# Attention and two MLPs in one kernel: the second MLP's rational function written as P·r·(2 − Q·r) in one PSUM bank, and the accumulators copied out in the step of their last matmul

## The chip, the cores and the metric

The kernel runs on one core of one Trainium2 chip. The metric is the device time of one execution in microseconds (us). An execution's span is the time from its first to its last instruction in the trace. Engines are named as in the profile: PE is TensorE's matmuls, PEld its weight loads, DVE is VectorE, ACT is ScalarE, POOL is GpSimd, SP issues the DMAs.

## The reference

```python
# q, k, v: (8, 8, 576, 64); x below: 4608 tokens x 512
q_s = softmax(q, axis=-1);  k_s = softmax(k, axis=2)
x = einsum(q_s, einsum('bhsd,bhse->bhde', k_s, v))      # to (4608, 512)
# first MLP (d_ff = 2048)
h = x @ moe_w_in
x = (h - tanh(h)) @ moe_w_out
# second MLP, a rational function of h
h = x @ moe2_w_in
P = a[0] + a[1]*h + a[2]*h*h + a[3]*h*h*h
Q = 1.0 + abs(b[0])*abs(h) + abs(b[1])*h*h
return (P / (Q + 1e-06)) @ moe2_w_out
```

## The kernel before

Tokens are worked in 9 blocks (index j, NBLK) of 512, and the 2048 hidden features in 16 slices (index f, KF) of 128. The first MLP is phase 1 and the second is phase 2; each is one loop of 144 steps (n), a step being one slice of one block. Every product is made from float32r parts: a value is split into a high part (h) and a low part (l), and `mm3` issues high·high, high·low and low·high. So `first_product` is 12 matmuls into one PSUM bank `hps` (four chunks c of the input, three matmuls each), and `second_product1` or `second_product2` is 12 matmuls into the four accumulators `acc0` to `acc3` (three in a row each). The order of each engine's instructions is written by hand: an engine runs its own list in program order, and semaphores hold it where it needs another engine's result.

In step n the PE list has the first product of n and then the second product of n−2 (LAG1 and LAG2 are 2), which is taken from `due`. Between the two products of one slice stands the nonlinearity.

Phase 1: ACT makes tanh into `t` (L668), DVE subtracts (L669), ACT rounds to `gh` (L237) and POOL makes `gl` (L238). Beside it run the attention of the next block (functions named kv_ and q_, spread over the steps by `front`, `turn` and `follow`), and, in `park`, the decoding of phase 2's weights.

Phase 2, with one line per instruction of 128×512: ACT makes |b0 h| into the PSUM tile `rx` (L623) and h² into `h2` (L624); DVE makes `qq` = |b1|h² + rx (L625); ACT makes the numerator's two linear pieces `n1` and `n0` (L631, L632); POOL makes n1·h2 (L633) and n0 + n1 (L634). ACT makes a first reciprocal r in `rx` (L606, L607). DVE refines it by one Newton step (L611, L612), multiplies it by the numerator (L615), rounds that to `gh` (L237) and subtracts for `gl` (L238). The reciprocal and everything behind it of slice n is issued in step n+1.

At the end of a block two more pieces of work come up. In the step f = 15, `next_x` splits the next block's input: ACT rounds four chunks to `xh` (L224) and DVE subtracts for four chunks `xl` (L225), ahead of that step's other work. One step and a half later, after the last second product of the block, the closure `leave` copies `acc0` and `acc2` out on ACT (L570 in phase 1, L587 in phase 2) and `acc1` and `acc3` on DVE (L571, L588), and SP stores them. `leave` is returned by the second product, is called in the next step (under the name `end`), and the next block's second product can write an accumulator only when its copy is done.

Of the kernel before, what the change touches and what calls it, by code (L numbers as in the profile page):

```python
# [8 lines left out]
F32 = mybir.dt.float32  # L9
F32R = mybir.dt.float32r  # L10
# [4 lines left out]
AF = mybir.ActivationFunctionType  # L15
ALU = mybir.AluOpType
AX = mybir.AxisListType

P = 128
NB = 512  # L20
NEG = -3.0e38
EPS_S = 1e-9
ONE_EPS = 1.0 + 1e-6

SK = 32
LAG1 = 2
LAG2 = 2
# [3 lines left out]
def attention_moe_moe2_kernel(ctx, tc, q, k, v, w1, w2, w3, w4, ca, cb, out):  # L31
# [11 lines left out]
    NBLK = NT // NB  # L43
    NPAIR = H // 2
    KC = DM // P
# [8 lines left out]
    gp = ctx.enter_context(tc.tile_pool(name="gp", bufs=2))  # L54
# [5 lines left out]
    PE, ACT, DVE, POOL, SP = nc.tensor, nc.scalar, nc.vector, nc.gpsimd, nc.sync  # L60

    def f32(ap):
        return ap.bitcast(F32)
# [142 lines left out]
    def unpark(which, f):  # L206

        d = parked[which, f]
        for i, w in enumerate(place((which, f))):
            SP.dma_start(out=f32(w), in_=d[:, i])  # L210
# [7 lines left out]
    xh, xl = (xp.tile([P, KC, NB], F32R, tag=f"x{part}", name=f"x{part}") for part in "hl")  # L218
    xr = xp.tile([P, KC, NB], F32, tag="xr", name="xr")

    def next_x():

        for c in range(KC):
            ACT.copy(out=xh[:, c, :], in_=xr[:, c, :])  # L224
            DVE.tensor_tensor(out=xl[:, c, :], in0=xr[:, c, :], in1=f32(xh[:, c, :]), op=ALU.subtract)  # L225

    def first_product(f):
        hps = ps_h.tile([P, NB], F32, tag="h", name="hps")
# [2 lines left out]
            mm3(hps, wh, wl, xh[:, c, :], xl[:, c, :], c == 0, c == KC - 1)  # L231
        return hps

    def split(g, on_dve):
        gh = gp.tile([P, NB], F32R, tag="gh", name="gh")
        gl = gp.tile([P, NB], F32R, tag="gl", name="gl")
        (DVE.tensor_copy if on_dve else ACT.copy)(out=gh, in_=g)  # L237
        (DVE if on_dve else POOL).tensor_tensor(out=gl, in0=g, in1=f32(gh), op=ALU.subtract)  # L238
        return gh, gl

    acc = {}
# [245 lines left out]
    def follow(after):  # L487
        for fn in [late for fn in after for late in [fn()] if late]:
            fn()
# [21 lines left out]
    with tc.manual_schedule():  # L511
# [47 lines left out]
        def second_product1(j, f, gh, gl):  # L559
            if f == 0:  # L560
                new_acc()
            wh, wl = wb(f)
            for m in range(4):
                c = slice(m * P, (m + 1) * P)
                mm3(acc[m], wh[:, c], wl[:, c], gh, gl, f == 0, f == KF - 1)

            def leave(acc=dict(acc)):
                for m in range(0, 4, 2):
                    st = leaving()
                    ACT.copy(out=st[:, 0], in_=acc[m])  # L570
                    DVE.tensor_copy(out=st[:, 1], in_=acc[m + 1])  # L571
                    SP.dma_start(out=x2d[j][:, m:m + 2], in_=st)

            return leave if f == KF - 1 else None

        def second_product2(j, f, gh, gl):
            if f == 0:
                new_acc()
            wh, wl = wb(f)
            for m in range(4):  # L580
                c = slice(m * P, (m + 1) * P)
                mm3(acc[m], gh[:, c], gl[:, c], wh, wl, f == 0, f == KF - 1)

            def leave(acc=dict(acc)):
                for m in range(0, 4, 2):
                    st = leaving()
                    ACT.copy(out=st[:, 0], in_=acc[m])  # L587
                    DVE.tensor_copy(out=st[:, 1], in_=acc[m + 1])  # L588
                    rows = out[j * NB:(j + 1) * NB, :].rearrange("(p g) m -> p g m", g=4)
                    SP.dma_start(out=rows[:, m:m + 2], in_=st)  # L590

            return leave if f == KF - 1 else None
# [8 lines left out]
        ahead = const.tile([P, 1], F32, name="ahead")  # L601
        DVE.memset(bias_q, ONE_EPS * 2.0**-SK)

        def rational_seed(x, qq):

            ACT.activation(out=x, in_=qq, func=AF.Abs_reciprocal_sqrt, scale=2.0**-SK, bias=bias_q)  # L606
            ACT.activation(out=x, in_=x, func=AF.Square, scale=2.0 ** (-SK / 2))  # L607

        def rational_step(x, qq):

            DVE.scalar_tensor_tensor(out=qq, in0=qq, scalar=ONE_EPS, in1=x, op0=ALU.add, op1=ALU.mult)  # L611
            DVE.scalar_tensor_tensor(out=x, in0=qq, scalar=2.0, in1=x, op0=ALU.subtract, op1=ALU.mult)  # L612

        def rational_end(x, n0):
            DVE.scalar_tensor_tensor(out=n0, in0=n0, scalar=-1.0, in1=x, op0=ALU.mult, op1=ALU.mult)  # L615
            return split(n0, True)

        def rational_open(hps):

            x = ps_a.tile([P, NB], F32, tag="a", name="rx")  # L620
            h2 = rp.tile([P, NB], F32, tag="h2", name="h2")
            qq = rp.tile([P, NB], F32, tag="qq", name="qq")
            ACT.activation(out=x, in_=hps, func=AF.Abs, scale=b0)  # L623
            ACT.activation(out=h2, in_=hps, func=AF.Square)  # L624
            DVE.scalar_tensor_tensor(out=qq, in0=h2, scalar=b1, in1=x, op0=ALU.mult, op1=ALU.add)  # L625
            return x, h2, qq

        def rational_top(hps, h2):
            n1 = rp.tile([P, NB], F32, tag="n1", name="n1", bufs=1)
            n0 = rp.tile([P, NB], F32, tag="n0", name="n0")  # L630
            ACT.activation(out=n1, in_=hps, func=AF.Identity, scale=a3, bias=a2)  # L631
            ACT.activation(out=n0, in_=hps, func=AF.Identity, scale=a1, bias=a0)  # L632
            POOL.tensor_tensor(out=n1, in0=n1, in1=h2, op=ALU.mult)  # L633
            POOL.tensor_tensor(out=n0, in0=n0, in1=n1, op=ALU.add)  # L634
            return n0


        STEPS = NBLK * KF
        due = {}
        last = STEPS - KF  # L640
        rat = leave = None
        for n in range(2 * STEPS + LAG2 + 1):
            ph, j, f = n // STEPS, n % STEPS // KF, n % KF
            end, leave = leave, None
            if n < STEPS:
                front(work[n])
                hps = first_product(f)
                if end:
                    end()
                if f == KF - 1 and j + 1 < NBLK:  # L650
                    next_x()
                if n == last:
                    ACT.activation(out=absb, in_=coef[:, 4:6], func=AF.Abs)
                    att.release()
                    outp = ctx.enter_context(tc.tile_pool(name="outp", bufs=2, side="right"))
                    load_x2(0)
                if n >= last:
                    unpark("a", f)
                if f == KF - 1 and n > last:
                    next_x()  # L660
                    load_x2(1)
                if n in due:
                    leave = due.pop(n)()
                if n >= last + LAG1:
                    unpark("b", f - LAG1)
                after = turn(work[n])
                t = gp.tile([P, NB], F32, tag="t", name="t", bufs=1)
                ACT.activation(out=t, in_=hps, func=AF.Tanh)  # L668
                DVE.tensor_tensor(out=t, in0=hps, in1=t, op=ALU.subtract)  # L669
                ph_w, turns = None, 0  # L670
                if j == 0:
                    ph_w, turns = 0, 1 if f % 4 == 2 else 2
                due[n + LAG1] = lambda a=(j, f, *split(t, False)): second_product1(*a)
                if turns:
                    decode(ph_w, True)
                follow(after)
                if turns > 1:
                    decode(ph_w, False)
                if KF - 1 <= n < KF + PACE * (2 * KF + 1):
                    park(n - KF)  # L680
                if n == STEPS - 1:

                    ACT.activation(out=ahead, in_=bias_q, func=AF.Abs_reciprocal_sqrt)
            else:
                if n == STEPS:
                    rp = ctx.enter_context(tc.tile_pool(name="rp", bufs=2, side="right"))
                old, rat = rat, None
                if n < 2 * STEPS:
                    hps = first_product(f)
                    if f == KF - 1 and j + 1 < NBLK:  # L690
                        next_x()
                        if j + 2 < NBLK:
                            load_x2(j + 2)
                leave = due.pop(n)() if n in due else None
                if n < STEPS + LAG1:
                    unpark("b", KF - LAG1 + f)
                if old:
                    rational_seed(*old[0])
                if end:
                    end()  # L700
                if old:
                    rational_step(*old[0])
                if n < 2 * STEPS:
                    x, h2, qq = rational_open(hps)
                    rat = ((x, qq), rational_top(hps, h2), (j, f))
                if old:
                    due[n + LAG2 - 1] = lambda a=(*old[2], *rational_end(old[0][0], old[1])): second_product2(*a)


# [28 lines left out]
```

## Time and profile before

| | before |
|---|---|
| runs | 1741.19, 1742.47, 1742.45 us; median 1742.45 |
| profiled execution | 1741.09 us; span 1739.3 us |
| PE busy | 1686.4 us, 97% of the span |
| PEld, DVE | 1389.8 us (80%), 1221.4 us (70%) |
| ACT, POOL | 978.6 us (56%), 674.1 us (39%) |
| chain that ended last | PE 84%, DVE 11%, issue 3%, ACT 1% |

The busy shares are means over both phases. In phase 1 (up to about 930 us) DVE is busy about half of the time; in phase 2 (from about 930 us) over nine tenths. An idle bracket in the rows below, as [0.95 <-DVE gl L238], is the time that the engine sat idle before the instruction and who ended the wait. Names in the rows leave out buffer numbers, and matmuls of several weight slices can share a name.

### The profile page before, as it was taken

How to read it: one execution, taken by the hardware profiler on the slowest of the kernel's cores; microseconds unless marked ns; L12 is line 12 of the kernel's file. 1: busy time of each engine (PE TensorE's matmuls, PEld its weight loads, DVE VectorE, ACT ScalarE, POOL GpSimd, SP SyncE). 2: the span in 40 equal slices, each digit the busy share in tenths (PEclk: the TensorE clock that was granted, in tenths of full speed). 3: DMA queues.
4: the chain of work that ended last, by engine and by line, in shares of the span. 5: the costliest groups of instructions: out<-in, count | busy, mean ns of one | idle time of the engine just before them, and what ended most of it. 6: DMA issues, size and time to landing. Idle time of an engine off the chain costs nothing.

```text
span 1739.3 us, 21473 instructions
## 1 busy us (share of the span) xinstructions
PE 1686.4 (97%) x7640; PEld 1389.8 (80%) x7640; DVE 1221.4 (70%) x1785; ACT 978.6 (56%) x1656; POOL 674.1 (39%) x544
## 2 busy tenths in 40 slices
PE   5899999999999999999999999999999999999998
PEld 3677888888888888888888878787878787878786
DVE  7997445455444545432215999999999999999997
ACT  5666444444444444432325676767676767676765
POOL 3443323233222323233223444444444444444443
PEclk8899999999999999999999999999999999999999
DMA  7552433333332333210354010101010101000000
GB/s 214 159 161 69 135 95 112 94 105 106 100 98 89 119 100 106 74 55 1 131 194 159 0 49 1 49 1 49 1 49 1 49 1 46 4 31 19 1 25 24
DMA packets 108763, 125.13 MB, mean 72 GB/s; under 512 B 48624, under 2 KB 82416, under 8 KB 107504
## 3 DMA queue, kind: packets, MB, share of 16 engines
q1 hardware_dynamic: 108656, 123.76, 22.2%
q8 instruction: 60, 0.98, 0.2%
q14 instruction: 47, 0.39, 0.1%
HBM read 88.08 MB, written 35.65 MB: 71 GB/s over the span
## 4 chain that ended last, share of the span: by engine, by line
PE 84%; DVE 11%; issue 3%; ACT 1%; SPq 0%; DMA 0%; DVEq 0%; ACTq 0%
PE acc L68 14%; PE acc L66 13%; PE acc L67 13%; PE hps L68 13%; PE hps L66 13%; PE hps L67 13%; PE kvps L359 2%; DVE e L134 1%; DVE m L135 1%; DVE xl L225 1%; DVE m L122 1%; DVE gl L238 1%; PE qps L442 1%; DVE n L615 1%; DVE gh L237 1%
## 5 line engine op out<-in xcount | busy, mean ns | idle before, releaser
L238 POOL TENSOR_TENSOR gl<-t,gh 128x512 fp32r<-128x512 f32 x144 | 187.6, 1303 | 546.9 <-ACT gh L237 546.9
L633 POOL TENSOR_TENSOR n<-n,h 128x512 f32<-128x512 f32 x144 | 186.5, 1295 | 404.0 <-ACT n L631 404.0
L237 ACT CAST gh<-t 128x512 fp32r<-128x512 f32 x144 | 89.4, 621 | 291.5 <-PE acc L68 267.2
L669 DVE TENSOR_TENSOR t<-hps,t 128x512 f32<-128x512 f32 x144 | 98.9, 687 | 217.0 <-ACT t L668 217.0
L238 DVE TENSOR_TENSOR gl<-n,gh 128x512 fp32r<-128x512 f32 x144 | 213.9, 1485 | 13.7
L623 ACT ACTIVATE rx<-hps,coef 128x512 f32<-128x512 f32 x144 | 95.3, 662 | 210.0 <-PE hps L68 210.0
L634 POOL TENSOR_TENSOR n<-n,n 128x512 f32<-128x512 f32 x144 | 193.7, 1345 | 11.3
L668 ACT ACTIVATE t<-hps 128x512 f32<-128x512 f32 x144 | 85.9, 596 | 160.2 <-PE hps L68 159.7
L237 DVE CAST gh<-n 128x512 fp32r<-128x512 f32 x144 | 119.5, 830 | 14.1 <-PE acc L68 0.5
L625 DVE SCALAR_TENSOR_TENSOR qq<-h,absb,rx 128x512 f32<-128x512 f32 x144 | 107.5, 746 | 27.3 <-ACT h L624 14.7
L66 PE MATMUL hps<-xh,wa2h 128*128 128x512 f32 x288 | 115.5, 401 | 0.0
L68 PE MATMUL hps<-xh,wa3l 128*128 128x512 f32 x288 | 112.6, 391 | 2.9 <-DVE wa3l L146 2.9
L66 PE MATMUL hps<-xh,wa1h 128*128 128x512 f32 x288 | 115.1, 400 | 0.0
L66 PE MATMUL hps<-xh,wa3h 128*128 128x512 f32 x288 | 114.5, 398 | 0.0
L66 PE MATMUL hps<-xh,wa0h 128*128 128x512 f32 x288 | 114.4, 397 | 0.0
L632 ACT ACTIVATE n<-hps,coef 128x512 f32<-128x512 f32 x144 | 113.7, 789 | 0.0
L67 PE MATMUL hps<-xl,wa0h 128*128 128x512 f32 x288 | 113.0, 392 | 0.0
L68 PE MATMUL hps<-xh,wa0l 128*128 128x512 f32 x288 | 112.8, 392 | 0.0
L68 PE MATMUL hps<-xh,wa2l 128*128 128x512 f32 x288 | 112.5, 391 | 0.0
L67 PE MATMUL hps<-xl,wa2h 128*128 128x512 f32 x288 | 112.5, 391 | 0.0
L67 PE MATMUL hps<-xl,wa1h 128*128 128x512 f32 x288 | 112.4, 390 | 0.0
L631 ACT ACTIVATE n<-hps,coef 128x512 f32<-128x512 f32 x144 | 112.4, 780 | 0.0
(227 smaller groups left out, 4565.5 us busy)
## 6 DMA issues: line engine op xcount, KB each, us to landing
raw<-in_moe_w_in_dram SPq DMA_DIRECT2D x32, 512.0 KB, 4.2
raw<-in_moe_w_out_dram SPq DMA_DIRECT2D x32, 512.0 KB, 4.1
xr<-x2d SPq DMA_DIRECT2D x9, 1024.0 KB, 4.7
out_dram<-st SPq DMA_DIRECT2D x18, 512.0 KB, 2.7
kt<-in_k_dram SPq DMA_DIRECT2D x32, 256.0 KB, 2.9
vt<-in_v_dram SPq DMA_DIRECT2D x64, 128.0 KB, 3.0
x2d<-raw SPq DMA_DIRECT2D x14, 512.0 KB, 3.2
qr<-in_q_dram SPq DMA_DIRECT2D x8, 256.0 KB, 3.3
```

Of the source, the lines that this page charges most:

```text
L66: PE.matmul(o, lhi, rhi, start=start, stop=False)
L67: PE.matmul(o, lhi, rlo, start=False, stop=False)
L68: PE.matmul(o, llo, rhi, start=False, stop=stop)
L237: (DVE.tensor_copy if on_dve else ACT.copy)(out=gh, in_=g)
L238: (DVE if on_dve else POOL).tensor_tensor(out=gl, in0=g, in1=f32(gh), op=ALU.subtract)
L623: ACT.activation(out=x, in_=hps, func=AF.Abs, scale=b0)
L625: DVE.scalar_tensor_tensor(out=qq, in0=h2, scalar=b1, in1=x, op0=ALU.mult, op1=ALU.add)
L631: ACT.activation(out=n1, in_=hps, func=AF.Identity, scale=a3, bias=a2)
L632: ACT.activation(out=n0, in_=hps, func=AF.Identity, scale=a1, bias=a0)
L633: POOL.tensor_tensor(out=n1, in0=n1, in1=h2, op=ALU.mult)
L634: POOL.tensor_tensor(out=n0, in0=n0, in1=n1, op=ALU.add)
L669: DVE.tensor_tensor(out=t, in0=hps, in1=t, op=ALU.subtract)
```

## The change

Four things are rewritten.

1. The rational function. `rx` holds in turn |b0 h|, Q, Q·r and the quotient; `qq` is gone. The reciprocal's first value r goes to an SBUF tile `r`. POOL multiplies the numerator by r, DVE makes x = (Q + 1e-6)·r and then x = (x − 2)·n0 in the same PSUM bank; the coefficients of the numerator are negated once. DVE rounds the bank to `gh` and subtracts for `gl` from the bank. `n1` has two buffers. The reciprocal's ACT instructions and the product with r are issued in the slice's own step, behind the numerator; the last product and the split in the next step.
2. In the last step the numerator's three POOL instructions run on DVE.
3. In phase 2 `next_x` gives the subtractions of chunks 2 and 3 to POOL.
4. `leave` is called in the step of the last matmul, behind the split. In phase 2 all four copies are DVE's, save in the last block.

```diff
-    def next_x():
+    def next_x(low=None):
         for c in range(KC):
             ACT.copy(out=xh[:, c, :], in_=xr[:, c, :])
-            DVE.tensor_tensor(out=xl[:, c, :], in0=xr[:, c, :], in1=f32(xh[:, c, :]), op=ALU.subtract)
+            eng = (low or [DVE] * KC)[c]
+            eng.tensor_tensor(out=xl[:, c, :], in0=xr[:, c, :], in1=f32(xh[:, c, :]), op=ALU.subtract)
...
-                    ACT.copy(out=st[:, 0], in_=acc[m])
+                    (ACT.copy if j == NBLK - 1 else DVE.tensor_copy)(out=st[:, 0], in_=acc[m])
...
-            DVE.scalar_tensor_tensor(out=qq, in0=h2, scalar=b1, in1=x, op0=ALU.mult, op1=ALU.add)
...
+        def rational_q(x, h2):
+            DVE.scalar_tensor_tensor(out=x, in0=h2, scalar=b1, in1=x, op0=ALU.mult, op1=ALU.add)
+        def rational_seed(x):
+            r = rp.tile([P, NB], F32, tag="r", name="r")
+            ACT.activation(out=r, in_=x, func=AF.Abs_reciprocal_sqrt, scale=2.0**-SK, bias=bias_q)
+            ACT.activation(out=r, in_=r, func=AF.Square, scale=2.0 ** (-SK / 2))
+            return r
+        def rational_step(x, r, n0, eng):
+            eng.tensor_tensor(out=n0, in0=n0, in1=r, op=ALU.mult)
+            DVE.scalar_tensor_tensor(out=x, in0=x, scalar=ONE_EPS, in1=r, op0=ALU.add, op1=ALU.mult)
+        def rational_end(x, n0):
+            DVE.scalar_tensor_tensor(out=x, in0=x, scalar=2.0, in1=n0, op0=ALU.subtract, op1=ALU.mult)
+        def split_end(x):
+            gh, gl = parts()
+            DVE.tensor_copy(out=gh, in_=x)
+            DVE.tensor_tensor(out=gl, in0=x, in1=f32(gh), op=ALU.subtract)
+            return gh, gl
...
+                    DVE.tensor_scalar(out=coef[:, 0:4], in0=coef[:, 0:4], scalar1=-1.0, scalar2=None, op0=ALU.mult)
...
                 follow(after)
+                if leave:
+                    leave()
...
+                eng = DVE if n == 2 * STEPS - 1 else POOL
...
-                        next_x()
+                        next_x((DVE, DVE, POOL, POOL))
...
+                if n < 2 * STEPS:
+                    x, h2 = rational_open(hps)
                 if old:
-                    rational_seed(*old[0])
-                if end:
-                    end()
-                if old:
-                    rational_step(*old[0])
+                    rational_end(*old[0])
                 if n < 2 * STEPS:
-                    x, h2, qq = rational_open(hps)
-                    rat = ((x, qq), rational_top(hps, h2), (j, f))
+                    rational_q(x, h2)
+                    n0 = rational_top(hps, h2, eng)
                 if old:
-                    due[n + LAG2 - 1] = lambda a=(*old[2], *rational_end(old[0][0], old[1])): second_product2(*a)
+                    due[n + LAG2 - 1] = lambda a=(*old[1], *split_end(old[0][0])): second_product2(*a)
+                if leave:
+                    leave()
+                if n < 2 * STEPS:
+                    rational_step(x, rational_seed(x), n0, eng)
+                    rat = ((x, n0), (j, f))
```

## Rows read from the trace of the kernel before

**Rows 1.** Windows, 200 us of phase 2: busy us (instructions) by engine, clock, DMA.
```profile
1200.00:1400.00 200.00, 198.09 (x870) 162.35 (x869) 185.72 (x233) 140.96 (x231) 94.56 (x73) 1.00 0.07 27
```
**Rows 2.** Timeline of PE in phase 2: start, duration, instruction, idle before it.
```profile
1109.95 0.50 PE L68 MATMUL acc<-wb3h,gl 128*128 128x512 f32 x1 [0.95 <-DVE gl L238]
...
1197.13 0.40 PE L67 MATMUL acc<-wb3l,gh 128*128 128x512 f32 x1
1198.48 0.50 PE L68 MATMUL acc<-wb3h,gl 128*128 128x512 f32 x1 [0.95 <-DVE gl L238]
1198.82 0.40 PE L66 MATMUL acc<-wb3h,gh 128*128 128x512 f32 x1
...
1714.48 0.39 PE L66 MATMUL hps<-xh,wa3h 128*128 128x512 f32 x1
...
1719.92 0.39 PE L66 MATMUL hps<-xh,wa3h 128*128 128x512 f32 x1
```
**Rows 3.** Waits of PE, 950 to 1735 us: total us, times, longest.
```profile
PE acc L68 <- DVE gl L238: 8.6, 9, 1.0
```
**Rows 4.** Waits of PEld and of PE, 130 to 945 us.
```profile
PEld acc L66 <- DVE raw L571: 7.5, 6, 1.7
...
PE acc L66 <- DVE raw L571: 5.0, 4, 1.3
```
**Rows 5.** Timeline of PE in phase 1, at one of those waits.
```profile
665.24 0.39 PE L68 MATMUL acc<-gh,wb0l 128*128 128x512 f32 x1
666.84 0.50 PE L66 MATMUL acc<-gh,wb0h 128*128 128x512 f32 x1 [1.21 <-DVE raw L571]
```
**Rows 6.** Timeline of DVE in the same place.
```profile
662.25 0.29 DVE L332 TENSOR_REDUCE mc<-kvps 128x1 f32<-128x128 f32 x1 [1.45 <-PE kvps L326]
...
666.10 1.28 DVE L571 COPY raw<-acc 128x512 f32<-128x512 f32 x2
```
**Rows 7.** Groups by line, 800 to 1700 us: count, busy us, mean ns, idle before.
```profile
L634 POOL TENSOR_TENSOR n<-n,n 128x512 f32<-128x512 f32 x139 | 186.9, 1345 | 10.9
...
L625 DVE SCALAR_TENSOR_TENSOR qq<-h,absb,rx 128x512 f32<-128x512 f32 x139 | 103.7, 746 | 26.7 <-ACT h L624 14.7
...
L612 DVE SCALAR_TENSOR_TENSOR rx<-qq,rx 128x512 f32<-128x512 f32 x138 | 95.9, 695 | 4.7
```
**Rows 8.** Instructions of single lines: ns lowest/median/highest, first and last start.
```profile
L238 POOL TENSOR_TENSOR gl<-t,gh x144: 1276/1294/1837, 50.5 to 930.7; 128x512 fp32r<-128x512 f32 x144
L238 DVE TENSOR_TENSOR gl<-n,gh x144: 691/1594/1667, 941.7 to 1730.8; 128x512 fp32r<-128x512 f32 x144
...
L237 DVE CAST gh<-n x144: 427/841/1323, 940.8 to 1730.2; 128x512 fp32r<-128x512 f32 x144
...
L615 DVE SCALAR_TENSOR_TENSOR n<-n,rx x144: 677/681/687, 940.1 to 1729.4; 128x512 f32<-128x512 f32 x144
...
L588 DVE COPY st<-acc x18: 675/677/691, 1031.9 to 1735.0; 128x512 f32<-128x512 f32 x18
```
**Rows 9.** Timeline of ACT: a block's end, and the last step of phase 2.
```profile
1189.46 2.67 ACT L224 CAST xh<-xr 128x512 fp32r<-128x512 f32 x4 [0.89 <-PE hps L68]
...
1722.84 0.66 ACT L623 ACTIVATE rx<-hps,coef 128x512 f32<-128x512 f32 x1 [1.73 <-PE hps L68]
...
1723.90 0.78 ACT L631 ACTIVATE n<-hps,coef 128x512 f32<-128x512 f32 x1
1724.56 0.79 ACT L632 ACTIVATE n<-hps,coef 128x512 f32<-128x512 f32 x1
...
1725.96 0.58 ACT L607 ACTIVATE rx<-rx 128x512 f32<-128x512 f32 x1
```
**Rows 10.** Timeline of PE over the last two second products.
```profile
1726.38 0.50 PE L66 MATMUL acc<-wb3h,gh 128*128 128x512 f32 x1 [0.86 <-DVE gh L237]
...
1734.60 0.39 PE L68 MATMUL acc<-wb3h,gl 128*128 128x512 f32 x1
```
**Rows 11.** Windows, a stretch inside them: columns as in the first group.
```profile
1729.00:1732.00 3.00, 3.00 (x9) 2.32 (x8) 2.14 (x4) 0.00 (x0) 0.00 (x0) 0.50 0.00 0
```

More of the change, by code (lines that the diff above doesn't have):

```diff
@@ L232, in first_product, with parts, split @@
         return hps
[L234 to L238, printed above, removed]
+    def parts():
+        return tuple(gp.tile([P, NB], F32R, tag=tag, name=tag) for tag in ("gh", "gl"))
+    def split(g):
+        gh, gl = parts()
+        ACT.copy(out=gh, in_=g)
+        POOL.tensor_tensor(out=gl, in0=g, in1=f32(gh), op=ALU.subtract)
         return gh, gl
@@ L602, in attention_moe_moe2_kernel @@
         DVE.memset(bias_q, ONE_EPS * 2.0**-SK)
[L604 to L616, printed above, removed]
         def rational_open(hps):
@@ L621, in rational_open, with rational_top @@
             h2 = rp.tile([P, NB], F32, tag="h2", name="h2")
-            qq = rp.tile([P, NB], F32, tag="qq", name="qq")
             ACT.activation(out=x, in_=hps, func=AF.Abs, scale=b0)
             ACT.activation(out=h2, in_=hps, func=AF.Square)
-            DVE.scalar_tensor_tensor(out=qq, in0=h2, scalar=b1, in1=x, op0=ALU.mult, op1=ALU.add)
-            return x, h2, qq
-        def rational_top(hps, h2):
-            n1 = rp.tile([P, NB], F32, tag="n1", name="n1", bufs=1)
+            return x, h2
+        def rational_top(hps, h2, eng):
+            n1 = rp.tile([P, NB], F32, tag="n1", name="n1")
             n0 = rp.tile([P, NB], F32, tag="n0", name="n0")
@@ L632, in rational_top @@
             ACT.activation(out=n0, in_=hps, func=AF.Identity, scale=a1, bias=a0)
-            POOL.tensor_tensor(out=n1, in0=n1, in1=h2, op=ALU.mult)
-            POOL.tensor_tensor(out=n0, in0=n0, in1=n1, op=ALU.add)
-            return n0
+            eng.tensor_tensor(out=n1, in0=n1, in1=h2, op=ALU.mult)
+            eng.tensor_tensor(out=n0, in0=n0, in1=n1, op=ALU.add)
+            return n0
+        def rational_q(x, h2):
[11 more added lines that the diff above has]
+        def split_end(x):
+            gh, gl = parts()
+            DVE.tensor_copy(out=gh, in_=x)
+            DVE.tensor_tensor(out=gl, in0=x, in1=f32(gh), op=ALU.subtract)
+            return gh, gl
         STEPS = NBLK * KF
@@ L640, in attention_moe_moe2_kernel @@
         last = STEPS - KF
-        rat = leave = None
+        rat = None
         for n in range(2 * STEPS + LAG2 + 1):
             ph, j, f = n // STEPS, n % STEPS // KF, n % KF
-            end, leave = leave, None
+            leave = None
             if n < STEPS:
@@ L672, in attention_moe_moe2_kernel @@
                     ph_w, turns = 0, 1 if f % 4 == 2 else 2
-                due[n + LAG1] = lambda a=(j, f, *split(t, False)): second_product1(*a)
+                due[n + LAG1] = lambda a=(j, f, *split(t)): second_product1(*a)
                 if turns:
@@ L696, in attention_moe_moe2_kernel @@
                     unpark("b", KF - LAG1 + f)
+                if n < 2 * STEPS:
+                    x, h2 = rational_open(hps)
                 if old:
-                    rational_seed(*old[0])
-                if end:
-                    end()
+                    rational_end(*old[0])
+                if n < 2 * STEPS:
+                    rational_q(x, h2)
+                    n0 = rational_top(hps, h2, eng)
                 if old:
-                    rational_step(*old[0])
+                    due[n + LAG2 - 1] = lambda a=(*old[1], *split_end(old[0][0])): second_product2(*a)
+                if leave:
+                    leave()
                 if n < 2 * STEPS:
-                    x, h2, qq = rational_open(hps)
-                    rat = ((x, qq), rational_top(hps, h2), (j, f))
-                if old:
-                    due[n + LAG2 - 1] = lambda a=(*old[2], *rational_end(old[0][0], old[1])): second_product2(*a)
+                    rational_step(x, rational_seed(x), n0, eng)
+                    rat = ((x, n0), (j, f))
 _INS = ["q", "k", "v", "moe_w_in", "moe_w_out", "moe2_w_in", "moe2_w_out", "moe2_a", "moe2_b"]
```

## The prediction
> **What bounds the kernel now.** First the windows, to see which engine is full in phase 2: PE is busy 198.1 of 200 us at clock 1.00 and DVE 185.7 [rows 1]. DVE looks nearly as full, so the next question is what PE's missing 1% is. The timeline of PE says it: within a block the first matmul of one product comes 5.44 us after that of the step before, 24 matmuls at 0.227 us with no gap, but once in a block PE stands 0.95 us before the third matmul of a second product, for gl of DVE, and two such stops are 88.53 us apart [rows 2]. Sixteen steps of 5.44 are 87.04, so a block's end costs 1.5 us: 0.95 of idle, a matmul after a wait that takes 0.50 instead of 0.39, and two shorter waits of the weight loads. The list of waits gives nothing else in phase 2: nine waits, 8.6 us in all, of which eight are block ends and one is the end of the kernel [rows 3]. So PE bounds phase 2 except at block ends, and a DVE freed elsewhere buys nothing. All that phase 2 holds, at an unchanged matmul rate, is 8 × 1.5 = 12 us, and something at the end.
>
> Phase 1 has waits of its own: PE for DVE's copy of an accumulator, four times, 5.0 us, and six waits of the weight loads [rows 4]. At one of them the next matmul starts 1.60 us after the one before instead of 0.23 [rows 5]: with the longer matmul behind it about 1.5 us.
>
> **Phase 1, the copies.** There DVE ends the small reduction L332 at 662.54, and copies only at 666.10; decoding and two reductions of the next step stand between [rows 6]. The change calls the copies right behind that reduction. The accumulators' matmuls are over by then, so both DVE copies are done near 663.8. The first accumulator that PE lacked was wanted at 665.47 (665.24 + 0.23), the last 1.4 later. The wait goes with 2 us to spare. What is late next: the work put back by 1.2 us feeds no matmul within a step, and L669 behind it keeps its place, since the same work stands ahead of it; SP stores earlier, and its loads queue behind a copy already running. Gain: 4 × 1.5 = 6.0, and for the two waits that only PEld shows 0.25 each: **6.5 us**. Lowest value 5 (the idle alone), highest 7.
>
> **An ordinary step of phase 2.** Zero is the start of ACT's L623. *DVE before*: 0.75 (Q) + two Newton instructions near 0.69 + 0.68 + 0.84 + 1.59, some 5.2 of 5.44 [rows 7, 8]. *After*: Q still 0.75; two instructions with one PSUM and one SBUF operand that write PSUM, the form of L612, 0.695 each; the rounding from PSUM like L588, 0.68; gl with one PSUM and one SBUF operand. For that one bounds: L615 has those operands and takes 0.677 to 0.687 in all 144 cases, many beside POOL's work, while gl from two SBUF operands takes 0.69 to 1.67. I take 0.69, the nearer form. Sum 3.5 us. *POOL*: a third instruction of 1.3 to 1.35, so 3 × 1.33 + 0.1 = 4.1 of 5.44. *ACT*: the same six, r now written to SBUF instead of PSUM; at most 0.04 more (SBUF to SBUF as L224, about 0.62, against 0.58 of L607) [rows 9].
>
> The chain: n1 ends at 1.84, n0 at 2.51, r at 3.74 (from the four rows of the last step) [rows 9]. POOL multiplies and adds from 1.92 to 4.62 and multiplies by r until 6.03, which is 0.59 in the next step. There DVE makes the end at 0.63 to 1.32, Q to 1.98, gh to 2.58, gl to 3.31. PE wants gh at 5.24 and gl at 5.69: over 2 us early, where gl before was 0.5 early. All of it is cover; gain and cost **0** in 136 steps. The negated coefficients and the second n1 buffer cost nothing, off every path.
>
> Two rules of the Trainium skill speak against parts of this. Its page VectorE: DVE Perf Modes, section "Why PSUM operands drop a tier", says that an fp32 operand in PSUM holds a copy at one element per cycle. The rows put a price on it: 0.677 from PSUM (L588) against 0.427 at best from SBUF [rows 8]; by the rule gh gets 0.25 dearer. The median from SBUF is 0.841, so by the median it gets 0.16 cheaper. In the ordinary step either hides under those 2 us, and the sum stays. ScalarE: Activation LUTs, section "Step-by-step: what each stage is for", says that ACT writes PSUM faster than SBUF; the 0.04 above is the bound by rows, and no run here shows r alone.
>
> **A block's end.** ACT's four xh end at 0.62, 1.30, 1.99 and 2.67 [rows 9], and L623 starts at 2.58, all of ACT 2.58 late. DVE does xl 0 and 1 to 2.02 and the end of the slice before to 2.64. POOL does xl 2 at 2.07 to 3.36 and xl 3 to 4.61; PE wants the last at 4.79, so that holds with 0.18 to spare. h² comes at 3.75, Q at 4.54, gh at 5.13, gl at 5.86. PE wants gh at 5.24 and its weight load 0.22 sooner; gl 0.17 late. Twice the 0.11 of a matmul after a wait [rows 2], 0.17: 0.4. Then POOL is the late one: n1·h2 can start at 4.56, so 5.86, 7.27 and 8.68; DVE's end waits for it to 9.44 with the next Q queued behind it to 10.1, then gh 10.7, gl 11.4. PE wants them at 10.7 and 11.1 plus the 0.4 already lost: just in time, 0.1 more. So 0.5 of the 1.5 stays, 1.0 is gained: 8 × 1.0 = **8 us**. Bounds: 12 if nothing stays; if POOL's instructions take the 1.35 of L634 throughout, 0.8 stays and the gain is 5.6.
>
> The copies of a finished block fall two steps later on DVE: four in a row at 0.60 apart, behind a gl that ends near 15.5, so the last ends at 17.9. PE wants acc0 at 16.6 and acc3 at 18.7: hidden. With that cover gone, each 0.1 would cost 0.8 us over the kernel.
>
> **The end.** In the last step DVE takes over the two numerator instructions, ahead of the split of slice 286: end 1.32, Q 1.98, the two to 3.3, gh 3.9, gl 4.6. PE wants gh at 2.52 and waits 1.4 us; before it waited 0.86 and 0.95 for gh and gl [rows 3, 10]. Then n0·r 5.2, x 5.8, end 6.5, gh 7.3, gl 8.0, and the last matmul starts at 10.2, against 11.76 before (1734.60 − 1722.84) [rows 10]: 1.6 gained. But behind those two waits the clock was at 0.50 from 1729 to 1732, half speed, seven matmuls at about 0.43 [rows 11], 1.4 us; at a block end, with one wait of 0.95, it stays at 1.00 [rows 1, 2]. The new waits sum to about as much as the old. If the last forecast matmuls run at half speed too, 0.2 is left. I take **0.8**, between them.
>
> **Sum.** 6.5 + 8 + 0.8 = 15.3. The profiled execution took 1741.09 (span 1739.3 and 1.8 around it): 1725.8. The median of the runs is 1.36 above it; half of that is added, **1726.5 us**. This kernel can tell a change of 0.2%, 3.5 us.
>
> **The rivals.**
> *Block ends keep their wait.* POOL's queue of five instructions, or a gl that still takes 1.59 beside POOL, leaves 1.2 to 1.5 of stall. For it: POOL works without a break from 2.07 to 8.7. Against: L615's 0.687 at most [rows 8]. Then 6.5 + 0.8 + 0 to 2.4: about 1733.5. Chance 0.2.
> *Block ends close wholly and the clock holds at the end.* 6.5 + 12 + 1.6 = 20.1: 1721.5. Against it, gl's 0.17. Chance 0.1.
> *GpSimd becomes the bound: slower.* Three instructions and 0.09 us of gaps fill 5.44 at 1.78 us each. The longest subtraction on POOL took 1.837 [rows 8]: 5.60 a step, 0.16 × 144 = 23 us in place of phase 2's gain, less phase 1's 6.5: 1758. For it: 1.837 was seen. Against: L634's mean of 1.345 in phase 2 itself [rows 7], and DVE loses its two-SBUF instruction there. It decides from 1.78 on. Chance 0.05.
> *The gains meet a new wait.* The copies on DVE, or the late end behind POOL, stop PE about 1 us more at each block's end than forecast, and an earlier phase 1 waits for its own attention work instead: near 1741. Chance 0.07.
> The forecast, 1723 to 1730 by itself, has 0.58.
>
> Eight times in ten: from the whole closing to the kept waits, 1721 to 1735. Faster by over 0.2%: 0.58 + 0.2 + 0.1 less a little, 0.87; within 0.2%: 0.07; slower: 0.06.
>
> **What would show it.** Right: no wait for L571's copies in phase 1; DVE's gl near 0.69 with DVE busy about 70% in phase 2; stops 87.5 us apart instead of 88.53; POOL near 75%. Wrong: gl near 1.6, POOL instructions over 1.4, PE waiting for an accumulator's copy, or stops still 88.5 apart.

## The result, and the profile after

The changed kernel takes 1722.1 us (median of 4 runs, 1721.42 to 1723.06) against 1741.99 us (4 runs) on the same chip: a ratio of 0.9887, with a 95% interval of 0.987 to 0.9904. The forecast was 1726.5 with a range of 1721 to 1735. The sign and the places are those of the forecast, and the gain is a quarter larger: in the profiled executions 1741.09 became 1721.89, 19.2 us where the sum said 15.3.

Where they went is read from one instruction that both kernels have 144 times, ACT's |b0 h| at the head of each step of phase 2. Its first start ends phase 1, its last start begins the end of the kernel. The first line is of the kernel before, the second of the one after (single instructions: ns lowest/median/highest, first and last start).

```profile
L623 ACT ACTIVATE rx<-hps,coef x144: 659/662/662, 932.7 to 1722.8; 128x512 f32<-128x512 f32 x144
```
```profile
L614 ACT ACTIVATE rx<-hps,coef x144: 653/662/663, 926.9 to 1704.8; 128x512 f32<-128x512 f32 x144
```

| stretch, us | before | after | difference | forecast |
|---|---|---|---|---|
| up to phase 2 | 932.7 | 926.9 | −5.8 | −6.5 |
| first to last step of phase 2 | 790.1 | 777.9 | −12.2 | −8 |
| last step to the end of the span | 16.5 | 15.3 | −1.2 | −0.8 |

143 steps in 777.9 us are 5.44 us each: phase 2 now runs at the pace of its matmuls from the first step to the last. The windows and the waits of the changed kernel say the same (busy us and instructions of PE, PEld, DVE, ACT, POOL; then total us, times, longest).

```profile
1200.00:1400.00 200.00, 200.00 (x885) 165.58 (x884) 134.67 (x198) 141.80 (x229) 149.35 (x115) 1.00 0.07 26
```
```profile
PE acc L66 <- DVE gh L647: 1.5, 2, 1.3
```

PE is busy all of the 200 us, DVE 135 of them instead of 186, POOL 149 instead of 95 [rows 1]. Between 945 and 1735 us PE waits twice, both times for gh in the last two second products; the eight stops at block ends are gone [rows 2, 3]. In phase 1 no wait for an accumulator's copy is left [rows 4]: DVE now copies right behind the small reduction, at the place of rows 6.

```profile
657.93 0.29 DVE L335 TENSOR_REDUCE mc<-kvps 128x1 f32<-128x128 f32 x1 [1.45 <-PE kvps L329]
658.13 1.28 DVE L574 COPY raw<-acc 128x512 f32<-128x512 f32 x2
```

The costs of the new instructions are read from the groups by line, 950 to 1700 us (count, busy us, mean ns, idle before and what ended it).

```profile
L639 POOL TENSOR_TENSOR n<-n,r 128x512 f32<-128x512 f32 x138 | 180.6, 1308 | 13.0 <-ACT r L635 2.8
...
L640 DVE SCALAR_TENSOR_TENSOR rx<-rx,r 128x512 f32<-128x512 f32 x138 | 96.5, 699 | 49.0 <-ACT r L635 47.9
L643 DVE SCALAR_TENSOR_TENSOR rx<-rx,n 128x512 f32<-128x512 f32 x138 | 96.5, 699 | 184.7 <-POOL n L639 183.9
L648 DVE TENSOR_TENSOR gl<-rx,gh 128x512 fp32r<-128x512 f32 x138 | 95.5, 692 | 13.7 <-PE acc L68 0.5
L647 DVE CAST gh<-rx 128x512 fp32r<-128x512 f32 x138 | 94.4, 684 | 0.0
...
L635 ACT ACTIVATE r<-r 128x512 f32<-128x512 f32 x138 | 87.3, 633 | 4.4
```

The one to see is gl: 692 ns on average beside a POOL that is busier than before, where it took 1594 in the median [rows 8]. The DVE instructions that used to fill 5.2 us of a step now wait 1.3 us per step for POOL (183.9 us in all), which costs nothing: PE waits for gh in the last two products alone.

### The profile page after: what moved, and what is told of

Its sections match the earlier page's. It is cut to its first block, busy times and chain, and to the rows that moved or that the text cites. A ratio compares the mean times of both kernels' runs of the same rounds, so it can differ in the third digit from the quotient of the medians.

```text
span 1720.1 us, 21610 instructions
## 1 busy us (share of the span) xinstructions
PE 1679.3 (98%) x7640; PEld 1391.9 (81%) x7640; DVE 1003.6 (58%) x1645; ACT 976.5 (57%) x1640; POOL 873.8 (51%) x701
## 4 chain that ended last, share of the span: by engine, by line
PE 91%; DVE 5%; ACT 1%; issue 1%; SPq 1%; DMA 0%; POOL 0%; POOLq 0%; DVEq 0%; ACTq 0%
PE hps L68 14%; PE hps L66 14%; PE hps L67 14%; PE acc L68 14%; PE acc L66 14%; PE acc L67 14%; PE kvps L362 2%; DVE e L134 1%; DVE m L135 1%; PE qps L445 1%; DVE m L122 1%; PE xps L68 0%; PE xps L67 0%; PE xps L66 0%; DVE t L682 0%
## 5 line engine op out<-in xcount | busy, mean ns | idle before, releaser
L643 DVE SCALAR_TENSOR_TENSOR rx<-rx,n 128x512 f32<-128x512 f32 x144 | 100.7, 699 | 191.5 <-POOL n L639 190.6
L614 ACT ACTIVATE rx<-hps,coef 128x512 f32<-128x512 f32 x144 | 95.3, 662 | 205.0 <-PE hps L68 205.0
L639 POOL TENSOR_TENSOR n<-n,r 128x512 f32<-128x512 f32 x143 | 187.0, 1308 | 13.5 <-ACT r L635 3.1
L625 POOL TENSOR_TENSOR n<-n,n 128x512 f32<-128x512 f32 x143 | 184.8, 1292 | 11.2
L640 DVE SCALAR_TENSOR_TENSOR rx<-rx,r 128x512 f32<-128x512 f32 x144 | 100.7, 699 | 52.3 <-ACT r L635 51.2
L623 ACT ACTIVATE n<-hps,coef 128x512 f32<-128x512 f32 x144 | 113.6, 789 | 0.0
L67 PE MATMUL hps<-xl,wa3h 128*128 128x512 f32 x288 | 112.9, 392 | 0.0
L68 PE MATMUL hps<-xh,wa1l 128*128 128x512 f32 x288 | 112.4, 390 | 0.0
```

The lines of the kernel that those rows point to most:

```text
L67: PE.matmul(o, lhi, rlo, start=False, stop=False)
L68: PE.matmul(o, llo, rhi, start=False, stop=stop)
L625: eng.tensor_tensor(out=n0, in0=n0, in1=n1, op=ALU.add)
L639: eng.tensor_tensor(out=n0, in0=n0, in1=r, op=ALU.mult)
L640: DVE.scalar_tensor_tensor(out=x, in0=x, scalar=ONE_EPS, in1=r, op0=ALU.add, op1=ALU.mult)
L643: DVE.scalar_tensor_tensor(out=x, in0=x, scalar=2.0, in1=n0, op0=ALU.subtract, op1=ALU.mult)
```

## The experiments

All times are medians of runs on the same chip as runs of the kernel before, whose median was 1741.7 to 1742.05; ratios are to those, with their 95% intervals.

### The copies alone

The kernel before with `leave` called in the step of the last matmul, in both phases, and nothing else:

```diff
-                if end:
-                    end()
...
                 follow(after)
+                if leave:
+                    leave()
...
                     due[n + LAG2 - 1] = lambda a=(*old[2], *rational_end(old[0][0], old[1])): second_product2(*a)
+                if leave:
+                    leave()
```

> The kernel before, with one thing changed: leave is called in the step of the accumulators' last matmul (behind follow in phase 1, behind the split in phase 2), ACT and DVE still sharing the copies. Theory A (the parts add up and the copies matter in phase 1 alone): the six waits for DVE's copy in phase 1 go, 6 us; the waits for gl at the block ends of phase 2 stay, 88.5 us apart; time 1736 us, ratio 0.9966. Rival (the copies also set the block ends of phase 2): the distance of the block ends falls by 0.2 or more, time 1734 or less. Rival (the copies only move the wait to the attention's work in phase 1): 1741, ratio 1.00.

1735.03 us, 0.996 (0.9948 to 0.9973): 6.7 us. The waits of PE from 130 us on:

```profile
PE acc L68 <- DVE gl L238: 8.6, 9, 1.0
PE hps L68 <- DVE wa3l L146: 2.5, 1, 2.5
PE acc L66 <- DVE gh L237: 0.9, 1, 0.9
```

The waits for the copies are gone, those for gl stand at their old 8.6 us, and the block ends are still 88.55 us apart (ACT's first `xh` copy starts at 1006.21 and 1094.76). Both rivals fall: the copies matter in phase 1 alone, and their wait is not handed on to the attention. (In phase 2 of the kernel before, ACT's copies of the accumulators start 18 us behind its `xh` copies, 1207.42 against 1189.46. That is a little over three steps, not one and a half.)

### The rational function alone

The changed kernel with the old place of the copies in phase 1, the top of the next step in phase 2, ACT sharing the copies and DVE making all four `xl`:

```diff
-                    (ACT.copy if j == NBLK - 1 else DVE.tensor_copy)(out=st[:, 0], in_=acc[m])
+                    ACT.copy(out=st[:, 0], in_=acc[m])
...
                 hps = first_product(f)
+                if end:
+                    end()
...
-                        next_x((DVE, DVE, POOL, POOL))
+                        next_x()
...
+                if end:
+                    end()
                 if n < 2 * STEPS:
                     x, h2 = rational_open(hps)
```

> The changed kernel with the old place of leave in phase 1 (the next step, behind the first product), the top of the next step in phase 2, ACT and DVE sharing the copies, and all four subtractions of next_x on DVE: the new rational function alone. Theory A: phase 1's six waits return, 6 us; phase 2 has no wait at its block ends: time 1728 us, 0.992 of before. Rival (phase 2 needs the copies or POOL's two subtractions too): waits at block ends of 0.5 to 1.5 us, 1732 to 1740.

1729.21 us, 0.9927 (0.9914 to 0.9939): 12.5 us. PE waits 5.0 us for the copies in phase 1 again, four times as before, and not once at a block end of phase 2, where the ends are 87.04 us apart (1100.46 and 1187.50). 6.7 and 12.5 make 19.2 of the 19.9 between the medians: the two parts add up, and they are the whole change within the noise of these medians.

### The two shifts of load, undone one at a time

`next_x()` instead of `next_x((DVE, DVE, POOL, POOL))`:

> The changed kernel with all four subtractions of next_x on DVE. Theory B (the high parts of the next block are copied chunk by chunk as soon as PE has done with that chunk, 2 us ahead of the product's end): gl of the slice before comes 0.4 us before PE wants it, no wait, time within 1 us of the changed kernel. Theory of the prediction (the copies start at the product's end): everything on DVE 1.8 us later, PE waits about 1.3 us at each of 8 block ends, 10 us slower.

1722.49 us (1722.02 to 1723.4). ACT instead of DVE for two of the four copies, in all blocks:

> The changed kernel with acc0 and acc2 copied by ACT in all blocks. Theory A: ACT has the room, the seed of that step comes 1 us later and the slack takes it: within 1 us of the changed kernel. Rival (ACT's copies ahead of the seed make POOL's product with r late, and the end behind it): 0.5 us at each of 8 blocks, 4 us slower, with PE waiting for gh or gl one step behind the copies.

1721.95 us (1720.86 to 1722.99). Neither differs from the changed kernel by more than the spread of its runs. Both lists have PE waiting in phase 2 only at the very end. POOL's two subtractions and DVE's four copies buy nothing here. The first of the two also speaks against a start of the `xh` copies at the product's end, from which 10 us of loss were expected.

### What made gl slow, from both sides

The kernel before with the quotient written to the bank, and gh and gl made from it:

```diff
-            DVE.scalar_tensor_tensor(out=n0, in0=n0, scalar=-1.0, in1=x, op0=ALU.mult, op1=ALU.mult)
-            return split(n0, True)
+            DVE.scalar_tensor_tensor(out=x, in0=n0, scalar=-1.0, in1=x, op0=ALU.mult, op1=ALU.mult)
+            return split(x, True)
```

> The kernel before with one line changed: the quotient is written to the PSUM bank and gh and gl are made from the bank; order, reciprocal, POOL and copies stay. Theory C: gl falls to 0.69 and gh to 0.68, DVE has 1 us more room per step, and the block end's wait falls from 1.5 to about 0.4: 8 us less, 1733 us. Rival (the new form of the rational function and its order make the block end, not the speed of gl): stops stay about 88.5 us apart, 1740 us.

1732.19 us, 0.9943 (0.993 to 0.9955): 9.9 us for one operand moved. Groups by line:

```profile
L238 DVE TENSOR_TENSOR gl<-rx,gh 128x512 fp32r<-128x512 f32 x137 | 94.8, 692 | 13.1
```

gl falls from a median of 1.59 to a mean of 0.69 with the order, the reciprocal and POOL's work left alone. The block ends are 87.52 us apart (1100.96 and 1188.48): 0.48 of the 1.5 stays, near the 0.4 that was expected, and PE's own list of waits has nothing but the last two products. ACT's first instruction of a step says where the gain lies:

```profile
L623 ACT ACTIVATE rx<-hps,coef x144: 658/662/663, 933.9 to 1715.6; 128x512 f32<-128x512 f32 x144
```

From the first to the last step of phase 2 it takes 781.7 us, 8.4 less than before, and from there to the end of the span (1730.4) 14.8, 1.7 less. Up to phase 2, where nothing was changed, this trace is 1.2 longer.

That POOL's work is what slows gl shows in the trace of the kernel before, in which gl has both operands in SBUF. 126 of its 144 gl overlap an instruction of POOL and take 1.58 to 1.67; the other 18 run while POOL is idle, and each takes 0.69. One of each kind, with POOL's list around them:

```profile
1189.67 1.60 DVE L238 TENSOR_TENSOR gl<-n,gh 128x512 fp32r<-128x512 f32 x1
1201.92 0.69 DVE L238 TENSOR_TENSOR gl<-n,gh 128x512 fp32r<-128x512 f32 x1
```
```profile
1189.36 1.36 POOL L634 TENSOR_TENSOR n<-n,n 128x512 f32<-128x512 f32 x1
...
1200.24 1.30 POOL L634 TENSOR_TENSOR n<-n,n 128x512 f32<-128x512 f32 x1
1205.72 1.30 POOL L633 TENSOR_TENSOR n<-n,h 128x512 f32<-128x512 f32 x1 [4.19 <-ACT n L631]
```

With the quotient in the bank, 143 of the 144 overlap POOL's work and all take 0.69.

The other way round, the changed kernel with the quotient in SBUF:

```diff
-            DVE.scalar_tensor_tensor(out=x, in0=x, scalar=2.0, in1=n0, op0=ALU.subtract, op1=ALU.mult)
+            DVE.scalar_tensor_tensor(out=n0, in0=x, scalar=2.0, in1=n0, op0=ALU.subtract, op1=ALU.mult)
...
-                    due[n + LAG2 - 1] = lambda a=(*old[1], *split_end(old[0][0])): second_product2(*a)
+                    due[n + LAG2 - 1] = lambda a=(*old[1], *split_end(old[0][1])): second_product2(*a)
```

> The changed kernel with the quotient written to n0 in SBUF instead of the bank, and gh and gl made from n0. Theory C (a DVE subtraction with both operands in SBUF runs at half speed beside POOL, one with an operand in PSUM doesn't): gl back at about 1.6 us and gh at 0.84 in an ordinary step, DVE one us busier per step; ordinary steps have the room, behind a block end gl comes 0.5 us late: 8 times 0.6, 1726 to 1728 us, with PE waiting for gl. Rival (gl was slow because of the long row of dependent DVE instructions around it): gl stays near 0.7, time as the changed kernel.

1738.18 us, 0.9978 (0.9969 to 0.9987): 16 us slower than the changed kernel, not 4 to 6. Groups by line, 950 to 1700 us, and the waits of the same execution:

```profile
L639 POOL TENSOR_TENSOR n<-n,r 128x512 f32<-128x512 f32 x135 | 216.1, 1601 | 11.1 <-POOL n L625 0.4
L648 DVE TENSOR_TENSOR gl<-n,gh 128x512 fp32r<-128x512 f32 x135 | 215.9, 1600 | 13.3 <-DVE gh L647 0.5
...
L647 DVE CAST gh<-n 128x512 fp32r<-128x512 f32 x135 | 156.5, 1159 | 0.0
```
```profile
PE acc L68 <- DVE gl L648: 7.6, 8, 1.0
...
PE acc L66 <- DVE gh L647: 5.1, 9, 1.4
```

The mechanism is the expected one, its size was short on two sides: gh goes to 1.16 (0.84 was taken from the kernel before, where POOL had fewer instructions), and POOL's own product with r goes from 1.31 to 1.60. So the chain through a block end gets longer at three places, PE waits for gh and for gl at each of the eight, and they are 89.09 us apart (1097.37 and 1186.46). With the split in SBUF the whole change would have kept 3.9 of its 20 us, less than the early copies bring alone.

### Both small parts together

The early copies and the quotient in the bank, on the kernel before; the old reciprocal, order and POOL work stay:

> The kernel before with two small parts of the change: the quotient in the PSUM bank with gh and gl made from it, and leave called in the step of the last matmul. The old reciprocal with its two Newton instructions, the old order, next_x and POOL's two instructions stay. Theory A and C: the two gains add, 6.7 and 9.9 of 1742: 1725.5 us; the rest of the change is then worth 3.5 us. Rival (they overlap at the block ends): 1729 or more.

1725.23 us, 0.9904 (0.989 to 0.9919). 6.7 and 9.9 are 16.6, and 16.4 is measured: they add. What the rest of the change brings beyond these two edits is 3 us. In the traces it is 3.8 us between the first and the last step of phase 2 (781.7 against 777.9), which is the 0.48 still lost at each of the eight block ends. From the last step to the end of the span this kernel, with the numerator of the last step left on POOL, takes 14.8 us and the changed kernel 15.3. So the bank alone brings the gain at the end; in the new order DVE's numerator is needed to keep it (16.7 us with product and sum on POOL, in the trace of the last experiment).

### Where the block end's copies start

The forecast kept 0.5 us at each block end, and none is there. Two kernels delay ACT's copies of the next block's high parts to where the forecast had them. First by their order:

```diff
-        for c in range(KC):
+        for c in (3, 0, 1, 2) if low else range(KC):
```

> The changed kernel, in phase 2 with next_x taking the chunks in the order 3, 0, 1, 2, so that ACT's first copy has to wait for the first product's last matmuls. Theory B (the prediction's block end was wrong only in where the copies start): ACT starts them 1.7 us later, gh and gl of two slices come late by what the prediction worked out, 0.3 to 0.6 us per block end, 1725 to 1727 us. Rival (the forecast's stall came from its durations or its order, not from that start): no wait, 1722.

1732.76 us (1731.12 to 1733.59), 10.7 over the changed kernel. The direction is the expected one, but the list of PE's waits in phase 2 shows another wait in it:

```profile
PE hps L67 <- DVE xl L226: 5.5, 8, 0.7
```

With chunk 3 first, chunk 0 comes second, and the next product wants its low part at its second matmul. The run thus mixes two delays and settles nothing alone. The second kernel keeps the order and holds the copies by one ACT instruction of one column:

```diff
+                        ACT.activation(out=ahead, in_=hps[:, 0:1], func=AF.Square)
                         next_x((DVE, DVE, POOL, POOL))
```

> The changed kernel, in phase 2 with one ACT instruction of one column that reads hps ahead of next_x: the copies of the high parts can't start before the first product's end, and their order stays 0, 1, 2, 3, so that nothing else moves (it costs 0.2 us itself). Theory B: this is the block end as the prediction drew it; gh and gl come 0.2 to 0.4 us late, 0.4 to 0.7 us of PE per block end, 1725.5 to 1728 us, and PE waits for gh and gl alone. Rival (the chunks' early start isn't what closed the block end): 1722 to 1723.

1723.88 us (1723.51 to 1725.04): 1.8 over the changed kernel's median, between what the theory and the rival expected. The two ranges don't meet, but they are of two chips, so the spacing is the firmer evidence. The block ends are 87.30 us apart (1096.67 and 1183.97) instead of 87.04, and at each a weight load waits for gl (timeline of PEld at one of them, and of ACT ahead of it):

```profile
1195.16 0.19 PEld L68 LDWEIGHTS acc<-wb3h,gl 128*128 128x128 f32 x1 [0.35 <-DVE gl L648]
```
```profile
1183.91 0.17 ACT L707 ACTIVATE ahead<-hps 128x1 f32<-128x1 f32 x1 [1.68 <-PE hps L68]
1183.97 2.17 ACT L224 CAST xh<-xr 128x512 fp32r<-128x512 f32 x4
1186.05 0.66 ACT L614 ACTIVATE rx<-hps,coef 128x512 f32<-128x512 f32 x1
```
```profile
1184.62 1.29 DVE L226 TENSOR_TENSOR xl<-xr,xh 128x512 fp32r<-128x512 f32 x2 [1.66 <-ACT xh L224]
...
1188.64 0.69 DVE L648 TENSOR_TENSOR gl<-rx,gh 128x512 fp32r<-128x512 f32 x1
```

So the late start costs 0.26 per block end, half of what the forecast kept. By the trace, the other half lies in the length of the copies: they take 2.17 us once they don't wait for PE, where the forecast had 2.67. L614 starts 2.14 us behind the product's end (1183.91, where the hold starts) instead of 2.58, and gl of the first slice ends 5.42 behind it (1189.33) instead of 5.86, ahead of the 5.69 at which PE wants it (its weight load starts at 1189.38). Only the gl of the second slice, behind POOL, is late. No run changes the length of the copies alone.

### The room on POOL

A fourth POOL instruction per step of phase 2, to a tile that nobody reads:

```diff
             eng.tensor_tensor(out=n0, in0=n0, in1=n1, op=ALU.add)
+            extra = rp.tile([P, NB], F32, tag="extra", name="extra", bufs=1)
+            POOL.tensor_tensor(out=extra, in0=n1, in1=h2, op=ALU.mult)
```

> The changed kernel with a fourth POOL instruction in every step of phase 2 (n1 times h2 once more, to a tile that nobody reads). Theory D (POOL has 1.3 us of room in an ordinary step and its two subtractions per block eat what is left): four instructions take 5.33 us of 5.44 and the block end adds 3, so POOL fills 88.5 us per block instead of 87.0 and becomes the bound: 1732 to 1737 us, PE waiting for gh or gl behind POOL in many steps. Rival (POOL's cover is wider, the queue recovers within a block): 1722 to 1724.

1745.82 us, 1.0021 of before (1.0012 to 1.003): 24 us slower than the changed kernel, and slower than the kernel before. Windows, with the columns as above, and waits:

```profile
1200.00:1400.00 200.00, 196.43 (x855) 159.44 (x855) 131.88 (x196) 141.25 (x223) 188.23 (x148) 1.00 0.07 27
```
```profile
POOL n L624 <- ACT n L622: 35.2, 110, 0.9
...
PE acc L66 <- DVE gh L649: 9.7, 10, 2.4
```

POOL is 94% busy, yet it is not the bound that was expected: in 110 steps it still waits for ACT. PE's waits are at block ends and at the end of the kernel: ten for gh (two of them in the last two products), and eight each for POOL's low parts and for DVE's copies of the accumulators; the ends are 89.8 us apart. By these waits, what was used up is the slack of a block end, not POOL's rate. Both the 1732 to 1737 that was expected and the rival's 1722 to 1724 are missed.

### The last step

In the changed kernel, the numerator's product and sum of the last step on POOL again, the product with r on DVE:

```diff
-                    n0 = rational_top(hps, h2, eng)
+                    n0 = rational_top(hps, h2, POOL)
```

> The changed kernel, in the last step with the numerator's product and sum left on POOL and only its product with r on DVE. Theory E (at the end of the kernel DVE's list of instructions in front of the last gh sets the time): PE waits for gh of the last slice but one 0.3 instead of 1.3 us, and the last gh comes 0.8 us sooner: 1721.2 us, 0.8 us less in the trace from the last first product to the end. Rival (the sum on POOL, 1.3 us each, comes later than DVE's): the last gh is no sooner, 1722 us or more.

1722.62 us (1721.56 to 1723.43): nothing gained. Timeline of PE in the last second product:

```profile
1712.07 0.50 PE L66 MATMUL acc<-wb3h,gh 128*128 128x512 f32 x1 [1.53 <-DVE gh L647]
...
1713.28 0.63 PE L66 MATMUL acc<-wb3h,gh 128*128 128x512 f32 x1
1713.71 0.63 PE L67 MATMUL acc<-wb3l,gh 128*128 128x512 f32 x1
```

And the windows of the same stretch, with the granted clock behind POOL's share:

```profile
1714.00:1716.00 2.00, 2.00 (x6) 1.52 (x6) 0.69 (x1) 0.11 (x1) 0.00 (x0) 0.50 0.00 0
```

The wait for the last gh but one is shorter as expected, but the last gh still waits for the sum on POOL, so PE's stop moves one product on; and behind a single stop of 1.53 us the matmuls come 0.43 us apart, at a granted clock of 0.50, which is 1.2 GHz. No version tried here is faster than the changed kernel by more than the spread of the runs.

## Why the prediction was right, and where its sum was short

**PE bounds phase 2 and only its waits can be gained: right.** The pace stayed at 5.44 us a step while DVE's load fell by a quarter. Of the signs named ahead, DVE at about 70% (135 of 200 us) and POOL near 75% (149) came; the stops 87.5 us apart didn't, since no stop was left.

**Phase 1, 6.5 us: right.** 5.8 in the trace, 6.7 with the copies alone.

**The ordinary step, 0: right, with its prices.** gl 0.692 (0.69), gh 0.684 (0.68), the two in-bank instructions 0.699 (0.695), POOL's third 1.31 (1.3 to 1.35), r 0.05 dearer for its place in SBUF (0.04). The chain came out too: in the timelines below, gl of the slice before ends at 1180.51, 3.36 us behind L614's start at 1177.15, where 3.31 was drawn. The Trainium skill's rule in VectorE: DVE Perf Modes, "Why PSUM operands drop a tier", holds as far as it goes: gh from PSUM never takes the 0.43 that SBUF allowed at best. But the bank's 0.684 is cheaper than the 0.841 median, and than the 1.16 that SBUF costs in the new kernel; the measurement decides for the bank.

**The block end, 8 us: the mechanism right, the term too small; 12.2 measured.** The step that failed is "ACT's four xh end at 0.62, 1.30, 1.99 and 2.67 [rows 9], and L623 starts at 2.58, all of ACT 2.58 late", which starts the copies at the end of the first product. The timeline of ACT and of PE in the changed kernel, at a block end:

```profile
1177.15 0.66 ACT L614 ACTIVATE rx<-hps,coef 128x512 f32<-128x512 f32 x1 [1.68 <-PE hps L68]
...
1180.28 0.63 ACT L635 ACTIVATE r<-r 128x512 f32<-128x512 f32 x1
1180.82 2.40 ACT L224 CAST xh<-xr 128x512 fp32r<-128x512 f32 x4
1183.12 0.65 ACT L614 ACTIVATE rx<-hps,coef 128x512 f32<-128x512 f32 x1
```
```profile
1180.13 0.39 PE L68 MATMUL hps<-xh,wa3l 128*128 128x512 f32 x1
...
1180.81 0.39 PE L68 MATMUL hps<-xh,wa3l 128*128 128x512 f32 x1
...
1181.49 0.39 PE L68 MATMUL hps<-xh,wa3l 128*128 128x512 f32 x1
...
1182.17 0.39 PE L68 MATMUL hps<-xh,wa3l 128*128 128x512 f32 x1
```

PE is done with a chunk of xh after the third matmul of that chunk. The first copy starts when ACT is done with r, 0.3 us behind the end of the first of these four and 1.7 us ahead of the product's end. The step's first own instruction, L614 here and L623 before, is therefore 0.5 late instead of 2.6 (1183.12; undisturbed it would start 5.44 behind the one of the step before, at 1182.59). The row that the forecast used had shown it: its copies began after a wait for PE of 0.89, at 1189.46 [rows 9], and PE's first chunk of that product ended at 1189.43:

```profile
1189.04 0.39 PE L68 MATMUL hps<-xh,wa3l 128*128 128x512 f32 x1
```

They lasted 2.67 us because PE frees a chunk every 0.68 (three times 0.68, and one copy of 0.62); the held-back copies take 2.17. With the copies held back, 0.26 of the forecast's 0.5 per block end returns, and as far as the trace of that run shows, the rest is the shorter copies.

**The queue on POOL, drawn as the late one: its order is right, its slack is not zero.** At the same place POOL and DVE show

```profile
1181.84 1.63 POOL L639 TENSOR_TENSOR n<-n,r 128x512 f32<-128x512 f32 x1
1183.43 3.00 POOL L226 TENSOR_TENSOR xl<-xr,xh 128x512 fp32r<-128x512 f32 x2
```
```profile
1179.82 0.69 DVE L648 TENSOR_TENSOR gl<-rx,gh 128x512 fp32r<-128x512 f32 x1
...
1181.55 2.47 DVE L226 TENSOR_TENSOR xl<-xr,xh 128x512 fp32r<-128x512 f32 x2
...
1190.44 0.70 DVE L643 SCALAR_TENSOR_TENSOR rx<-rx,n 128x512 f32<-128x512 f32 x1 [2.85 <-POOL n L639]
...
1192.50 0.69 DVE L648 TENSOR_TENSOR gl<-rx,gh 128x512 fp32r<-128x512 f32 x1
```

DVE waits 2.85 us for POOL's product, as drawn, and gl of that slice ends at 1193.19; PE starts that second product at 1193.27, loads gl as weights at 1193.50 and wants it in a matmul at 1193.73, so 0.3 us is left. Here the forecast was also lucky: it drew DVE's two xl in 1.4 us (0.62 to 2.02). They took 2.47, with POOL's product beside them, and cost nothing because they started 1.04 us ahead of the time that the forecast called zero (1182.59). Undoing either load shift stays within that; a fourth POOL instruction doesn't. That run is also the nearest that the slower rival came; its condition, POOL at 1.78 us an instruction, was not met: in the changed kernel the three average 1.29 to 1.31.

**The end, 0.8 us: 1.2 measured.** PE waited 1.34 and 0.18 us for gh, the forecast 1.4 and a little, and the granted clock held at 1.00, which is 2.4 GHz:

```profile
1708.00:1712.00 4.00, 3.08 (x12) 2.10 (x12) 3.76 (x7) 0.58 (x1) 0.00 (x0) 1.00 0.00 0
1712.00:1716.00 4.00, 3.51 (x13) 2.10 (x12) 1.93 (x4) 1.17 (x2) 0.00 (x0) 1.00 0.00 0
```

It also held in the other traces with a stop of 1.3 to 1.4 us at this place, and behind the 2.39 us of the run with a fourth POOL instruction. It fell to 0.50 behind the 0.86 and 0.95 of the kernel before, behind the same two stops with the copies alone, and behind the single 1.53 of the last experiment. So the length of the stop alone doesn't decide it; what does stays open.

**The rivals.** The sum came out as "block ends close wholly", given 0.1, whose 1721.5 was within 1 us; the forecast's own stretch, 1723 to 1730, was missed by 0.9. The errors of the three terms did not cancel: the 4.2 us of the block ends is nearly the whole difference. "Kept waits" hung on a gl that stays slow, or on POOL's queue. gl's operand had been priced rightly, and POOL's queue left 0.3 us.

## What to carry to other kernels

When one engine runs at its own pace except for a stop per block, look for the instruction on the way to that stop that takes twice its best time, and at what runs beside it: here one operand moved from SBUF to PSUM was worth 9.9 us, 8.4 of them out of the 12.2 in phase 2 and 1.7 at the end of the kernel. A buffer that is read in chunks can be released in chunks; a row of copies that begins after a short wait and goes on at the reader's pace has started early and is being fed, so its length isn't its cost. Where an accumulator's copy stands behind the next step's work, as on DVE in phase 1, it belongs in the step that finishes it; in phase 2 its place made no difference.

## What the runs showed of the hardware

DVE and POOL slow each other, not only one of them. With gh and gl made from SBUF beside three POOL instructions a step, gl took 1.60 instead of 0.69, gh 1.16 instead of 0.68, and POOL's product 1.60 instead of 1.31 (means of 135 and 138). In the changed kernel the same shows at block ends, where DVE's two `xl`, with both operands in SBUF, take 2.47 us beside POOL's product, which takes 1.63; in the held-back kernel, with POOL idle for all but the last 0.2 us, the pair took 1.29 us. With one operand in PSUM, gl took 0.69 whether POOL was busy or not. The page GPSIMD Engine Reference of the Trainium skill, "Key points", names the case: contention with DVE instructions that have two SBUF inputs, or that run in a 2-port perf mode. The rows of gl and xl agree with the first, and add that gl is then more than twice as long. gh has one SBUF input; whether it runs in such a mode no run here shows.
